# Attention and a gated MLP in one kernel: the passage from attention into the product sweeps is reordered and its loads are cut by heads

## The chip, the cores and the metric

The kernel runs on one core of a Trainium2 chip. The metric is device microseconds (us) of one execution. Three runs of the kernel before took 750.77, 751.29 and 752.87 us; the median is 751.29. The execution that the profiler recorded took 752.31 us, with a span of 750.5 us from the first to the last instruction (the other 1.8 us lie around it). All times below count from the start of that span.

## The reference

Attention with rotary position coding over 4 batches, 8 heads, 576 tokens and 64 values per head, then a gated MLP on the 2304 tokens (512 values wide, 1536 hidden).

```
q_rot, k_rot = rotate(q), rotate(k)
scores = softmax(q_rot @ k_rot.T / sqrt(64))
attn = scores @ v                                # [4, 8, 576, 64]
x = attn.transpose(0, 2, 1, 3).reshape(2304, 512)
out = (silu(x @ w_gate) * (x @ w_val)) @ w_out   # [2304, 512], float32
```

## The kernel before

**Numbers as pairs.** Each float32 operand of a matmul is split into a high part, rounded to the matmul's format by a copy on ScalarE (ACT), and a low part, the difference, made on VectorE (DVE) or GpSimd (POOL). A product is three matmuls: high by high, high by low, low by high. Such a copy and difference are a *split* (`split`).

**Stages.** Attention works through 16 head pairs, nine blocks each, until about 298 us. Each pair stores its unnormalised output (high and low halves added later) to a DRAM scratch `yd`, and each batch stores the reciprocals of its softmax sums to `rd`. The MLP works on transposed tokens, in six blocks of 384 (two halves `s` of three blocks `t`). It begins with 12 plain units of the first two hidden tiles (`UNITS`, functions `plain`, `mm`, `ev`; here u0 to u11): a unit is two chains of 12 matmuls (gate and value), each into one PSUM bank, then `ev` on ACT: Silu of the gate chain, a copy of the value chain into a staging buffer in SBUF, and a store to DRAM from ACT's queue. After the units come ten *sweeps* s (`strassen`), each with the weights of one pair of hidden tiles and three token pairs p in the order 1, 2, 0: a call of `unit` makes 7 chains of 6 matmuls instead of 8 by forming sums of operands ahead. Token pair p is blocks 2p and 2p+1; its sums are `T0`, `T1`, `T2`, its plain blocks `xa`, `xm`, `xb`. Then come the down projections (`finish`).

**The late tokens.** Blocks 0 to 3 are loaded and prepared during attention. Blocks 4 and 5 (s=1, t=1 and 2) need the last batch's last head pair. `yload(t)` loads the block's outputs into `Ya` (slot `T0h`) and `Yb` (slot `T2h`), all four head groups c at once; `rload` loads the reciprocals, spread over 64 partitions, into `R` or `R12` (slot `T2l`); `xlate(c, t)` adds, scales and splits one head group:

```
        x = self.aux()[:, 0:BK]
        ve.tensor_tensor(out=x, in0=Ya, in1=Yb, op=ALU.add)
        ve.tensor_tensor(out=x, in0=x, in1=self.R[1, t][:, c], op=ALU.mult)
        nc.scalar.copy(hi, x)
        nc.scalar.copy(Ya, x)
        ve.tensor_tensor(out=lo, in0=x, in1=r32(hi), op=ALU.subtract)
```

Units u8 and u9 read block 4, u10 and u11 block 5.

**Order.** In the MLP the order of PE, ACT, DVE and SP is the order of the code (a manual schedule); every engine runs its queue in order. `forms` (POOL) builds a token pair's sums, `forms2` (DVE) those of pair 2, from the copies of x that `xlate` leaves in `Ya`. A weight job (`Stream`, `bits`) is an Abs on ACT, six DVE operations (L721 to L726) and the next load; `J[s].sums` (POOL) and `J[s].split` make a sweep's weights. PE's chains rotate over six PSUM banks, so that a unit can start when `ev` of the unit three before has read its banks; two more banks are `aux`. The stores and loads use eight semaphore lanes; an issue waits for its lane's earlier DMA to land, and it holds its queue while it waits.

Of the kernel before, what the change touches and what calls it, by code (L numbers as in the profile page):

```python
# [14 lines left out]
ALU = mybir.AluOpType  # L15
# [503 lines left out]
class Moe:  # L519
    def __init__(self, tc, keep, pl, yd, rd, hd, wg, wv, wo, out):  # L520
        self.tc, self.nc = tc, tc.nc
        self.yd, self.rd, self.hd, self.w, self.wo, self.out = yd, rd, hd, (wg, wv), wo, out
        self.slot, self.xa, self.xm, self.xb, self.T = {}, {}, {}, {}, {}
        xs = keep.enter_context(tc.tile_pool(name="m_x", bufs=1))
        for blk in range(4):
            self.xbuf(xs, blk)
        pool = lambda name, bufs: pl.enter_context(tc.tile_pool(name=name, bufs=bufs, side="right"))
        one = pool("m_p", 1)
        self.Wb = [self.wbuf(one, 0), None]
        self.ld_p = pool("m_ld", 2)  # L530
        self.r_p = pool("m_r", 1)
# [45 lines left out]
    def open_late(self, ctx):  # L577
        def pool(name, bufs, **kw):
            return ctx.enter_context(self.tc.tile_pool(name=name, bufs=bufs, reuse_waits="tile", **kw))
        one = pool("m_late", 1)  # L580
        for blk in (4, 5):
            self.xbuf(one, blk)
        self.tbuf(one, 1)
        self.wform(one, 0)
        self.Ya = self.own(one, "T0h", [128, 2, 4, BK], FP32)
        self.Z2 = self.own(one, "T0l", [128, 2, 4, BK], FP32)
        self.Yb = self.own(one, "T2h", [128, 2, 4, BK], FP32)
        self.R12 = self.own(one, "T2l", [128, 2, 4, BK], FP32)[:, 0].rearrange("p c q -> p (c q)")
# [67 lines left out]
    def xlate(self, c, t):  # L656
        nc = self.nc
        ve = nc.vector
        hi, lo = self.xc(1, t, c)
        Ya, Yb = (Y[:, t - 1, c] for Y in (self.Ya, self.Yb))  # L660
        x = self.aux()[:, 0:BK]
        ve.tensor_tensor(out=x, in0=Ya, in1=Yb, op=ALU.add)  # L662
        ve.tensor_tensor(out=x, in0=x, in1=self.R[1, t][:, c], op=ALU.mult)
        nc.scalar.copy(hi, x)
        nc.scalar.copy(Ya, x)
        ve.tensor_tensor(out=lo, in0=x, in1=r32(hi), op=ALU.subtract)

# [110 lines left out]

    def gv(self, f, s, t):
        self.ev(f, s, t, [self.mm(f, s, t, i) for i in range(2)])  # L780

    def unit(self, fp, i, p):
# [9 lines left out]
        for k, (w, kind, x) in enumerate(PROD):  # L792
            acc = self.ch()[:, 0:BK]
            xh, xl = B[x] if kind == "B" else (Th[:, x], Tl[:, x])
            n = 0
            for c in range(2):
                for l, r in ((Wh, xh), (Wh, xl), (Wl, xh)):
                    nc.tensor.matmul(acc, l[:, w, c * 128:(c + 1) * 128], r[:, c], start=(n == 0), stop=(n == 5))  # L798
                    n += 1
# [84 lines left out]
    def hload(self, t):  # L884
        if t < FT + 2:
            self.HG[t % 2] = self.again(f"T0{'lh'[t % 2]}", [128, NFF, 2, 128], FP32, "hg")
        self.nc.sync.dma_start(out=self.HG[t % 2], in_=self.hd[1][t - FT])

    def hsplit(self, t):
# [3 lines left out]
        for z in range(0, NFF, 3):  # L893
            g, v = (G[:, z:z + 3, i] for i in range(2))
            ops.append(lambda g=g, v=v: self.nc.vector.tensor_tensor(out=g, in0=g, in1=v, op=ALU.mult))  # L895
# [45 lines left out]
def attn_swiglu(ctx: ExitStack, tc: tile.TileContext, qk, vr, wg, wv, wo, tab, out):  # L941
# [147 lines left out]
    moe.open_aux(xctx, 2)  # L1089
    J, S = plain(moe, ps)  # L1090
    mctx.close()
    pl.close()
    moe.open_mid(mctx)
    strassen(moe, J, S)
    xctx.close()
# [50 lines left out]
def plain(moe, ps):  # L1146
# [18 lines left out]
    S = Stream(moe, jobs)  # L1165
    st = {}

    def mix(p, c, Z):
        ops, st[p, c] = moe.forms(p, c, Z, po, ve)
        run(ops)  # L1170

    S.load()
    S.load()
    moe.yload(1)
    moe.rload(1, 1)
    S.sign()
    for c in range(2):
        mix(1, c, moe.Z2[:, c])
    for u, x in enumerate(UNITS):
        if u == 0:  # L1180
            moe.ev(*x, ps)
        else:
            moe.gv(*x)
        if u < 4:
            run(S.take(1, u < 3))
        if u == 1:
            run(J[0].sums(po))
            moe.yload(2)
            moe.rload(1, 2, moe.R12)
        if u in (2, 3):  # L1190
            run(st[1, u - 2])
        if u == 3:
            run(J[0].split(0, po))
            mix(0, 0, moe.again("raw0", [128, 4, BK], FP32, "Z"))
        if u == 4:
            run(J[0].split(1, po))
        if 4 <= u < 8:
            for c in range(2):
                moe.xlate(2 * u % 4 + c, u // 2 - 1)
        if u == 5:  # L1200
            mix(0, 1, moe.rz())
        if u == 7:
            moe.tagain(2)
            ops, st[2] = moe.forms2(ve, ve)
            run(ops)
            run(J[1].sums(po))
        if u == 8:
            run(st[2])
            moe.tagain(0)
        if u in (9, 10):  # L1210
            run(moe.split(ve, *(t[:, :, u - 9] for t in moe.T[0]), st[0, u - 9]))
        if u == 10:
            S.sign()
            run(S.take(1))
    return J, S

# [3 lines left out]

def strassen(moe, J, S):
    nc = moe.nc
# [88 lines left out]
```

## Time and profile before

| | us |
|---|---|
| profiled execution | 752.31 |
| its span | 750.5 |
| median of three runs | 751.29 |
| PE busy (share of the span) | 707.7 (94%) |
| DVE, POOL, ACT busy | 553.2, 460.2, 402.9 |
| first matmul of the first sweep, token pair 2 | 381.99 |

The page gives busy time per engine, then the span in 40 slices of 18.8 us, where a digit is the busy share in tenths and PEclk is the granted TensorE clock in tenths of 2.4 GHz. Then come queues, the chain of work that ended last, and groups of instructions by source line. Since PE is busy nearly everywhere, the place to look is the one where its digits fall: slices 16 to 20, from about 300 to 385 us.

### The profile page before, as it was taken

The numbers are of one execution on the slowest core, as the hardware profiler recorded it, in microseconds if no ns is written. First come the engines' busy times: TensorE is split into PE (matmuls) and PEld (weight loads), VectorE is DVE, ScalarE is ACT, GpSimd is POOL, SyncE is SP. The second block draws the span as 40 slices with busy tenths as digits, with TensorE's granted clock in tenths as the row PEclk, the third lists the DMA queues.
The fourth block names the chain that finished last, engine by engine and source line by source line (L and its number), as shares of the span: only waits on it lengthen the run. The fifth ranks groups of instructions, "written<-read, shape, count | busy, mean of one in ns | idle before, by whom it ended". The sixth has DMA issues, their size and how long they took to land.

```text
span 750.5 us, 12677 instructions
## 1 busy us (share of the span) xinstructions
PE 707.7 (94%) x4356; PEld 663.2 (88%) x4356; DVE 553.2 (74%) x895; ACT 402.9 (54%) x878; POOL 460.2 (61%) x462
## 2 busy tenths in 40 slices
PE   7699999999999998776889999999999999999997
PEld 6599999999999998775789999999999977788887
DVE  5799988888888887477686777878767885445541
ACT  2689888888889885243543342434333333333331
POOL 5696988899999846929146555676655766400000
PEclk9899999999999999987999999999999999999999
DMA  5878788889878893991236465555637965678661
GB/s 166 215 191 214 202 223 212 209 210 256 224 192 206 208 245 113 249 233 42 78 97 183 141 199 166 169 160 163 183 115 207 322 261 197 242 259 270 217 206 34
DMA packets 109873, 144.12 MB, mean 192 GB/s; under 512 B 17504, under 2 KB 86128, under 8 KB 108400
## 3 DMA queue, kind: packets, MB, share of 16 engines
q1 hardware_dynamic: 105104, 137.51, 64.0%
q10 hardware_dynamic: 4704, 5.79, 2.4%
q8 instruction: 35, 0.57, 0.3%
q14 instruction: 30, 0.25, 0.1%
HBM read 76.61 MB, written 42.54 MB: 159 GB/s over the span
## 4 chain that ended last, share of the span: by engine, by line
PE 64%; DVE 14%; DMA 11%; ACT 6%; issue 2%; POOL 2%; SPq 1%; ACTq 0%; DVEq 0%; POOLq 0%
PE ch L798 27%; PE ch L908 12%; PE pv L476 8%; PE sc L360 8%; PE tr L436 6%; DMA HF<-hf 2%; DVE nmt L375 2%; DVE aux L662 2%; PE tr L299 2%; DMA T0h<-yd 1%; ACT E L393 1%; DMA raw<-in_moe_w_gate_dram 1%; DMA T2h<-yd 1%; POOL fl L674 1%; DMA R<-rd 1%
## 5 line engine op out<-in xcount | busy, mean ns | idle before, releaser
L375 DVE TENSOR_REDUCE nmt<-sc 128x1 f32<-128x576 f32 x144 | 107.9, 751 | 21.1 <-PE sc L360 19.7
L393 ACT ACTIVATE E<-sc,nmt 128x576 f32<-128x576 f32 x128 | 97.2, 760 | 7.9 <-DVE nmt L375 7.2
L786 POOL TENSOR_TENSOR u<-u,z 128x384 f32<-128x384 f32 x30 | 30.5, 1016 | 101.1 <-DVE sg L786 101.1
L436 PE MATMUL tr<-ident,E 128*128 128x128 f32 x512 | 77.3, 274 | 0.4 <-DVE N L322 0.4
L360 PE MATMUL sc<-QK 128*128 128x288 f32 x248 | 61.5, 330 | 5.6 <-ACT ET1h L437 2.9
L801 ACT COPY c<-ch 128x384 f32<-128x384 f32 x30 | 14.4, 481 | 95.7 <-PE ch L798 52.6
L436 PEld LDWEIGHTS tr<-ident,E 128*128 128x128 f32 x512 | 61.8, 141 | 2.3 <-PE tr L299 1.4
L224 POOL TENSOR_TENSOR t<-X,tabs 128x256 f32<-128x256 f32 (+1 forms) x90 | 51.9, 598 | 15.1 <-DMA X<-in_qk_dram 7.3
L360 PE MATMUL sc<-N,QZ 128*128 128x288 f32 x248 | 54.0, 300 | 1.2 <-DMA QZ<-N 1.2
L908 PE MATMUL ch<-Oh,hh 128*128 128x512 f32 (+1 forms) x144 | 54.1, 376 | 1.0 <-ACT o L873 1.0
L437 ACT CAST ET2h<-tr 128x512 fp32r<-128x512 f32 x80 | 47.0, 587 | 13.2 <-PE tr L436 13.2
L908 PE MATMUL ch<-Oh,hl 128*128 128x512 f32 (+1 forms) x144 | 53.9, 375 | 0.0
L908 PE MATMUL ch<-Ol,hh 128*128 128x512 f32 (+1 forms) x144 | 53.9, 374 | 0.0
L438 DVE TENSOR_TENSOR ET2l<-tr,ET2h 128x512 fp32r<-128x512 f32 x80 | 52.9, 682 | 0.5 <-ACT ET2h L437 0.5
L438 DVE TENSOR_TENSOR ET1l<-tr,ET1h 128x512 fp32r<-128x512 f32 x64 | 42.8, 685 | 7.5 <-ACT ET1h L437 7.4
L228 POOL TENSOR_TENSOR rot<-rot,t 128x512 f32<-128x512 f32 (+1 forms) x45 | 45.8, 1017 | 3.5
L674 ACT CAST hh<-hg 128x384 fp32r<-128x384 f32 x44 | 22.6, 514 | 47.2 <-DVE hg L895 47.1
L786 DVE TENSOR_TENSOR sg<-ch,u 128x384 f32<-128x384 f32 x60 | 33.4, 557 | 19.1 <-PE ch L798 17.3
L674 DVE TENSOR_TENSOR hl<-hg,hh 128x384 fp32r<-128x384 f32 x44 | 24.6, 559 | 30.9 <-ACT hh L674 30.9
L360 PEld LDWEIGHTS sc<-QK 128*128 128x128 f32 x248 | 38.6, 192 | 9.8 <-ACT E L393 4.8
L437 ACT CAST ET1h<-tr 128x512 fp32r<-128x512 f32 x64 | 36.4, 597 | 18.6 <-PE tr L436 15.3
L227 POOL TENSOR_TENSOR rot<-X,tabs 128x512 f32<-128x512 f32 (+1 forms) x45 | 45.8, 1017 | 0.0
(403 smaller groups left out, 2427.5 us busy)
## 6 DMA issues: line engine op xcount, KB each, us to landing
QK<-N SPq DMA_DIRECT2D x62, 288.0 KB, 4.9
hg<-ht SPq DMA_DIRECT2D x11, 1536.0 KB, 7.7
HF<-hf SPq DMA_DIRECT2D x12, 896.0 KB, 5.2
X<-in_qk_dram SPq DMA_DIRECT2D x15, 576.0 KB, 6.9
yd<-Y SPq DMA_DIRECT2D x31, 256.0 KB, 3.2
ht<-sg SPq DMA_DIRECT2D x20, 384.0 KB, 3.5
hf<-sg SPq DMA_DIRECT2D x20, 384.0 KB, 3.6
ht<-sg SPq DMA_DIRECT2D x20, 320.0 KB, 2.9
```

The costliest lines, as they stand in the source:

```text
L224: ins = e.tensor_tensor(out=sel(t2, u), in0=sel(x, w), in1=tb(Sn, u), op=ALU.mult)
L360: nc.tensor.matmul(ps[:, g, 0:288], l, rr[:, o + g * 288:o + (g + 1) * 288], start=(x == 0), stop=(x == len(terms) - 1))
L375: nc.vector.tensor_reduce(out=nmcol, in_=ps[:, :, 0:288], axis=AX.XY, op=ALU.max, negate=True)
L393: nc.scalar.activation(out=E.rearrange("p (a b) -> p a b", a=2), in_=ps[:, :, 0:288], func=ACTF.Exp, bias=nmcol, scale=1.0, accum_out=self ...
L436: nc.tensor.transpose(ps[:, c], E[:, o + c * 128:o + (c + 1) * 128], self.ident)
L437: nc.scalar.copy(dst[0], src)
L438: nc.vector.tensor_tensor(out=dst[1], in0=src, in1=r32(dst[0]), op=ALU.subtract)
L476: nc.tensor.matmul(st["ps"][:, 0:w], VS[:, sl, :], t, start=(x == 0), stop=(x == last))
L674: return [lambda: self.nc.scalar.copy(h, f), lambda: le.tensor_tensor(out=l, in0=f, in1=r32(h), op=ALU.subtract)]
L786: add = lambda e, out, in0, in1: e.tensor_tensor(out=out, in0=in0, in1=in1, op=ALU.add)
L798: nc.tensor.matmul(acc, l[:, w, c * 128:(c + 1) * 128], r[:, c], start=(n == 0), stop=(n == 5))
L908: self.nc.tensor.matmul(ps, l[:, f], r[:, z], start=(n == 0), stop=(n == 3 * NFF - 1))
```

## The change

It changes the stretch between attention and the first sweep, in these ways.

- `yload` takes a range of head groups. Groups 0 to 2 of both late blocks are loaded first, group 3 (the last head pair) after them; the reciprocals of both blocks follow before the next weight loads. `open_late` lists the slots in another order, by which `Ya`, `Yb` stand in memory that is free early.
- `xlate` makes a list of steps: ACT copies `Ya` into the PSUM bank, and the DVE's add has that bank and `Yb` as inputs. The first steps of group c+1 stand ahead of the last ones of group c. Three of the four subtractions of `forms2` become six of half the width with x still in PSUM (L677 to L680), one stays (L709).
- `ev` has four staging buffers: two from slot `raw0`, two from `Xab`.
- The splits of token pair 0's sums (`T0`) move from the plain units into the first sweep, and its low half is two tiles. POOL's sums of pair 0 stand after the weight splits.
- The order of evictions, splits and weight jobs is new. The first sweep takes two weight jobs instead of one, after its first token pair.
- `OX` lives in the tile `R`; `hload` loads each half of a tile by a DMA of its own.

```diff
-    def yload(self, t):
+    def yload(self, t, c0, c1):
...
-                self.nc.sync.dma_start(out=Y[64 * h:64 * h + 64, t - 1], in_=src[a])
+                self.nc.sync.dma_start(out=Y[64 * h:64 * h + 64, t - 1, c0:c1], in_=src[a, :, c0:c1])
...
+        def first(c):
+            x = xs[c] = self.aux()[:, 0:BK]
+            ac.copy(x, self.Ya[:, t - 1, c])
+            tt(out=x, in0=x, in1=self.Yb[:, t - 1, c], op=ALU.add)
+            tt(out=x, in0=x, in1=self.R[1, t][:, c], op=ALU.mult)
+
+        def rest(c):
+            x = xs.pop(c)
+            hi, lo = self.xc(1, t, c)
+            ac.copy(hi, x)
+            if t == 1 or c < 2:
+                ac.copy(self.Ya[:, t - 1, c], x)
+            tt(out=lo, in0=x, in1=r32(hi), op=ALU.subtract)
+            if t == 2 and c < 2:
+                tt(out=A[:, c], in0=x, in1=A[:, c], op=ALU.subtract)
+            elif t == 2:
+                tt(out=Bl[:, c - 2], in0=x, in1=Bl[:, c - 2], op=ALU.subtract)
+                tt(out=Bl[:, c], in0=x, in1=A[:, c - 2], op=ALU.subtract)
...
+    for t in (1, 2):
+        moe.yload(t, 0, 3)
+    for t in (1, 2):
+        moe.yload(t, 3, 4)
+        moe.rload(1, t, moe.R12 if t == 2 else None)
+    for c in range(2):
+        run(moe.forms(1, c, moe.Z[c], po))
+    x1, x2 = moe.xlate(1), moe.xlate(2)
+    mm(1)
+    S.sign()
+    ev(0)
+    mm(2)
+    run(S.take(1))
+    ev(1)
+    mm(3)
+    run(S.take(1, False))
+    run(J[0].sums(po))
+    ev(2)
+    mm(4)
+    T1(0)
+    run(x1, 3)
+    ev(3)
+    mm(5)
+    run(x1)
+    ev(4)
+    mm(6)
+    T1(1)
+    S.sign()
+    run(S.take(1, False))
...
+    run(w[0])
+    ev(5)
+    mm(7)
+    run(w[1])
+    run(x2, 3)
+    ev(6)
+    mm(8)
...
+    for c in range(2):
+        run(moe.forms(0, c, Z[c], po))
+    run(x2)
+    ev(7)
+    mm(9)
+    run(moe.forms2(ve))
+    ev(8)
+    mm(10)
+    S.sign()
+    ev(9)
+    mm(11)
+    run(S.take(1))
+    ev(10)
+    run(J[1].sums(po))
+    ev(11)
...
+    at(0, 0, 1, T0(1))
+    at(0, 0, 4, T0(0))
...
-        n = {0: 1, 2: 3, 4: 3, 6: 3}.get(s, 2)
+        n = {2: 3, 4: 3, 6: 3}.get(s, 2)
```

SP's queue before, from the last weight load of attention: `T0h`, `T2h` are the two halves of the late blocks, `R` the reciprocals; the brackets name what the issue waits for (DMAHW0 to DMAHW7 are the lanes).

```order
L738 DMA raw<-in_moe_w_val_dram 128x1024 [waits DMAHW0_49,Pool_49]
L654 DMA T0h<-yd 64x4x384 [waits DMAHW4_49,DMAHW3_49,DMAHW5_49,DMAHW2_49,DMAHW6_49,DMAHW1_49,DMAHW7_49,DVE_49,Activation_49]
L654 DMA T2h<-yd 64x4x384 [waits DVE_49]
L654 DMA T0h<-yd 64x4x384
L654 DMA T2h<-yd 64x4x384 [waits DMAHW0_49]
L630 DMA R<-rd 64x4x128 [waits Pool_49]
```

The same place of SP's queue with the change:

```order
L654 DMA T0h<-yd 64x3x384 [waits DMAHW5_49,DMAHW2_49]
L654 DMA T2h<-yd 64x3x384 [waits DMAHW3_49]
L654 DMA T0h<-yd 64x3x384 [waits DMAHW4_49]
L654 DMA T2h<-yd 64x3x384 [waits DMAHW6_49]
L654 DMA T0h<-yd 64x384 [waits DMAHW0_49]
L654 DMA T2h<-yd 64x384 [waits DMAHW1_49]
L654 DMA T0h<-yd 64x384 [waits DMAHW2_49]
L654 DMA T2h<-yd 64x384 [waits DMAHW3_49]
L630 DMA R<-rd 64x4x128 [waits DMAHW4_49,Pool_49]
```

Four loads of block 4 (groups 0 to 2, not shown) stand ahead of these, right behind the weight load, and wait for lanes 4, 6, 7 and 0 and for an earlier store. The shown ones are block 5's groups 0 to 2, block 4's group 3 and the first reciprocals; before, one block came whole, and its first load waited for every lane.

ACT's queue before, from the third eviction (L766, L767 and its stores L774, L777) on; L720 is the Abs of a weight job:

```order
L720 ACTIVATE aux<-raw 128x512
L766 ACTIVATE Xab<-ch 128x3x128
L767 COPY Xab<-ch 128x3x128
L774 DMA hf<-Xab 128x256
L777 DMA ht<-Xab 128x2x256
L720 ACTIVATE aux<-raw 128x512
L674 CAST T1h<-T0l 128x4x384
```

With the change (evictions are L779, L780, stores L787, L790, `sv` and `Xab` the staging buffers):

```order
L779 ACTIVATE Xab<-ch 128x3x128
L780 COPY Xab<-ch 128x3x128
L787 DMA hf<-Xab 128x256
L790 DMA ht<-Xab 128x2x256
L694 CAST T1h<-T0l_4436 128x4x384
L665 COPY aux<-T0h 128x384 x2
L672 CAST xa2h<-aux 128x384
L674 COPY T0h<-aux 128x384
L779 ACTIVATE Xab<-ch 128x3x128
```

No weight job stands between the second and the third eviction now; the first head group of block 4 stands ahead of the fourth.

DVE's queue before, where block 4 begins:

```order
L726 TENSOR_TENSOR WF_4439<-raw,aux 128x512
L674 TENSOR_TENSOR T1l<-T0l,T1h 128x4x384
L662 TENSOR_TENSOR aux<-T0h,T2h 128x384
L663 TENSOR_TENSOR aux<-aux,R 128x384
L666 TENSOR_TENSOR xa2l<-aux,xa2h 128x384
```

With the change:

```order
L694 TENSOR_TENSOR T1l<-T0l_4436,T1h 128x4x384
L666 TENSOR_TENSOR aux<-aux,T2h 128x384
L667 TENSOR_TENSOR aux<-aux,R 128x384
L666 TENSOR_TENSOR aux<-aux,T2h 128x384
L667 TENSOR_TENSOR aux<-aux,R 128x384
L675 TENSOR_TENSOR xa2l<-aux,xa2h 128x384
```

The add now has one input from PSUM (`aux`) and one from SBUF, and group 1's add and multiplication stand ahead of group 0's subtraction.

## Rows read from the trace of the kernel before

**Rows 1.** The page's slices: busy tenths of PE, granted clock.

```profile
PE   7699999999999998776889999999999999999997
...
PEclk9899999999999999987999999999999999999999
```

**Rows 2.** Windows: length, busy us (instructions) of PE, PEld, DVE, ACT, POOL; PEclk, DMA share, GB/s.

```profile
292.00:301.00 9.00, 8.77 (x55) 8.44 (x54) 4.45 (x9) 1.96 (x5) 5.75 (x6) 1.00 0.32 98
303.20:382.00 78.80, 58.84 (x283) 53.77 (x283) 54.20 (x64) 30.12 (x54) 41.21 (x34) 0.89 0.54 147
304.00:330.00 26.00, 21.98 (x116) 21.34 (x116) 14.22 (x20) 5.54 (x10) 15.50 (x15) 0.93 1.06 263
...
343.90:353.90 10.00, 6.54 (x17) 5.23 (x18) 7.49 (x8) 3.04 (x8) 8.82 (x6) 0.50 0.15 51
420.00:450.00 30.00, 30.00 (x175) 30.00 (x174) 23.72 (x42) 13.16 (x22) 18.03 (x18) 1.00 0.58 171
```

**Rows 3.** Timeline of PE: start, us, work, [idle before and its releaser]; units u2, u3, u4, sweep.

```profile
303.20 0.44 PE L758 MATMUL ch<-xa1h,w0h 128*128 128x384 f32 x1 [0.86 <-ACT Xab L766]
...
307.47 0.34 PE L758 MATMUL ch<-xa0h,w0h 128*128 128x384 f32 x1
...
311.63 0.34 PE L758 MATMUL ch<-xm0h,w0h 128*128 128x384 f32 x1
...
381.99 0.44 PE L798 MATMUL ch<-xa2h,W0h 128*128 128x384 f32 x1 [1.62 <-DVE u L786]
```

**Rows 4.** Waits of PE, 303.2 to 382.3: total us, times, longest.

```profile
PE ch L758 <- ACT Xab L766: 10.3, 5, 3.5
```

**Rows 5.** Line L654 (late blocks' loads) on SP: ns min/median/max, first to last start.

```profile
L654 SPq EVENT_SEMAPHORE  x4: 28/28/9209, 292.3 to 301.7; - x4
L654 SPq DMA_DIRECT2D T0h<-yd x4: 585/600/679, 301.8 to 314.2; - x4
```

**Rows 6.** DMA issues, 290 to 296 us: count, KB each, median us to landing.

```profile
raw<-in_moe_w_val_dram SPq DMA_DIRECT2D x1, 512.0 KB, 3.7
```

**Rows 7.** DMA issues, 300 to 320 us.

```profile
hf<-Xab ACTq DMA_DIRECT2D x2, 384.0 KB, 7.8
R<-rd SPq DMA_DIRECT2D x2, 256.0 KB, 9.3
```

**Rows 8.** Timeline of ACT and its queue.

```profile
305.39 0.33 ACTq L774 DMA_DIRECT2D hf<-Xab  x1
318.34 0.63 ACT L720 ACTIVATE aux<-raw 128x512 f32<-128x512 f32 x1 [12.97 <-DMA raw<-in_moe_w_val_dram]
```

**Rows 9.** Groups by line and shape, 303.2 to 382: busy us, mean ns, idle before.

```profile
L662 DVE TENSOR_TENSOR aux<-T0h,T2h 128x384 f32<-128x384 f32 x8 | 12.3, 1541 | 0.0
...
L766 ACT ACTIVATE Xab<-ch 128x384 f32<-128x384 f32 x11 | 5.4, 491 | 0.0
...
L665 ACT COPY T0h<-aux 128x384 f32<-128x384 f32 x8 | 3.9, 485 | 0.0
L691 DVE TENSOR_TENSOR T0h<-T0h 128x768 f32<-128x768 f32 x4 | 3.8, 956 | 0.1
...
L674 DVE TENSOR_TENSOR T1l<-T0l,T1h 128x1536 fp32r<-128x1536 f32 x2 | 3.5, 1757 | 2.9 <-ACT T1h L674 2.9
...
L726 DVE TENSOR_TENSOR WF<-raw,aux 128x512 f32<-128x512 f32 x5 | 3.4, 686 | 0.2
...
L674 ACT CAST T1h<-T0l 128x1536 fp32r<-128x1536 f32 x2 | 2.9, 1467 | 4.5 <-DMA T2l<-rd 4.5
...
L674 ACT CAST W0h<-WF 128x1024 fp32r<-128x1024 f32 x2 | 2.1, 1042 | 0.4 <-ACT Xab L767 0.4
```

**Rows 10.** Timeline of POOL at the first late add.

```profile
333.27 3.00 POOL L674 TENSOR_TENSOR W0l<-WF,W0h 128x1024 fp32r<-128x1024 f32 x1 [13.22 <-ACT W0h L674]
```

**Rows 11.** Timeline of DVE: the first and the last of eight late adds.

```profile
333.95 2.74 DVE L662 TENSOR_TENSOR aux<-T0h,T2h 128x384 f32<-128x384 f32 x1
...
359.74 0.56 DVE L662 TENSOR_TENSOR aux<-T0h,T2h 128x384 f32<-128x384 f32 x1
```

More of the change, by code (lines that the diff above doesn't have):

```diff
@@ L653, in yload, with xlate @@
             for a, Y in enumerate((self.Ya, self.Yb)):
-                self.nc.sync.dma_start(out=Y[64 * h:64 * h + 64, t - 1], in_=src[a])
-    def xlate(self, c, t):
+                self.nc.sync.dma_start(out=Y[64 * h:64 * h + 64, t - 1, c0:c1], in_=src[a, :, c0:c1])
+    def xlate(self, t):
         nc = self.nc
[L658 to L666, printed above, removed]
+        ve, ac = nc.vector, nc.scalar
+        tt = ve.tensor_tensor
+        A, Bl = self.Ya[:, 0], self.Ya[:, 1]
+        xs = {}
+        def first(c):
[15 more added lines that the diff above has]
+                tt(out=Bl[:, c], in0=x, in1=A[:, c - 2], op=ALU.subtract)
+        ops = [lambda: first(0)]
+        for c in range(4):
+            if c < 3:
+                ops.append(lambda c=c: first(c + 1))
+            ops.append(lambda c=c: rest(c))
+        return ops
     def hicopy(self, eng, out, in_):
@@ L793, in unit @@
             acc = self.ch()[:, 0:BK]
-            xh, xl = B[x] if kind == "B" else (Th[:, x], Tl[:, x])
+            if kind == "B":
+                xh, xl = B[x]
+            else:
+                xh, xl = Th[:, x], [t[:, x] for t in Tl] if isinstance(Tl, list) else Tl[:, x]
             n = 0
             for c in range(2):
-                for l, r in ((Wh, xh), (Wh, xl), (Wl, xh)):
-                    nc.tensor.matmul(acc, l[:, w, c * 128:(c + 1) * 128], r[:, c], start=(n == 0), stop=(n == 5))
+                rh, rl = xh[:, c], xl[c] if isinstance(xl, list) else xl[:, c]
+                for l, r in ((Wh, rh), (Wh, rl), (Wl, rh)):
+                    nc.tensor.matmul(acc, l[:, w, c * 128:(c + 1) * 128], r, start=(n == 0), stop=(n == 5))
                     n += 1
@@ L833, in of @@
         if 4 <= f < 4 + NX:
+            if self.OX is None:
+                self.OX = self.r_p.tile([128, NX, DM], FP32, name="R")
             return self.OX[:, f - 4]
@@ L885, in hload @@
         if t < FT + 2:
-            self.HG[t % 2] = self.again(f"T0{'lh'[t % 2]}", [128, NFF, 2, 128], FP32, "hg")
-        self.nc.sync.dma_start(out=self.HG[t % 2], in_=self.hd[1][t - FT])
+            if t % 2:
+                G = self.again("T0h", [128, NFF, 2, 128], FP32, "hg")
+                self.HG[1] = [G[:, 0:6], G[:, 6:NFF]]
+            else:
+                self.HG[0] = [self.again(f"T0l{x}", [128, 6, 2, 128], FP32, "hg") for x in range(2)]
+        for x, G in enumerate(self.HG[t % 2]):
+            self.nc.sync.dma_start(out=G, in_=self.hd[1][t - FT, :, 6 * x:6 * x + 6])
     def hsplit(self, t):
@@ L893, in hsplit @@
         for z in range(0, NFF, 3):
-            g, v = (G[:, z:z + 3, i] for i in range(2))
+            g, v = (G[z // 6][:, z % 6:z % 6 + 3, i] for i in range(2))
             ops.append(lambda g=g, v=v: self.nc.vector.tensor_tensor(out=g, in0=g, in1=v, op=ALU.mult))
@@ L1089, in attn_swiglu @@
     moe.open_aux(xctx, 2)
-    J, S = plain(moe, ps)
+    J, S, Z = plain(moe, ps)
     mctx.close()
@@ L1165, in plain, with mm, ev @@
     S = Stream(moe, jobs)
[L1166 to L1170, printed above, removed]
+    ps, sv = {0: ps}, {}
+    def mm(u):
+        f, a, t = UNITS[u]
+        ps[u] = [moe.mm(f, a, t, i) for i in range(2)]
+    def ev(u):
+        if u % 4 == 0:
+            raw = moe.again("raw0", [128, 2, 2 * BK], FP32, "sv")
+            sv[u], sv[u + 1] = raw[:, 0], raw[:, 1]
+        elif u % 4 > 1:
+            sv[u] = moe.ld_p.tile([128, 2, BK], FP32, name="Xab").rearrange("p a q -> p (a q)")
+        moe.ev(*UNITS[u], ps.pop(u), sv.pop(u))
@@ L1172, in plain, with T1 @@
+    def T1(c):
+        run(moe.split(ve, *(t[:, :, c] for t in moe.T[1]), moe.Z[c]))
     S.load()
     S.load()
-    moe.yload(1)
-    moe.rload(1, 1)
-    S.sign()
-    for c in range(2):
[L1178 to L1214, printed above, removed]
@@ new lines, in plain @@
+    ev(4)
[3 more added lines that the diff above has]
+    run(S.take(1, False))
+    w = [J[0].split(x, po) for x in range(2)]
+    run(w[0])
[5 more added lines that the diff above has]
+    mm(8)
+    Z = [moe.r_p.tile([128, 4, BK], FP32, name="R"), moe.again("T0l0", [128, 4, BK], FP32, "Z")]
+    for c in range(2):
+        run(moe.forms(0, c, Z[c], po))
[9 more added lines that the diff above has]
+    run(S.take(1))
@@ L1227, in at, with T0, go @@
         own.setdefault((s, q, k), []).extend(f)
+    Th, Tl = moe.T[0] = [moe.again("T0h", [128, 4, 2, BK], F32R, "T0h"), [None, None]]
+    def T0(c):
+        def go():
+            Tl[c] = moe.again(f"T0l{c}", [128, 4, BK], F32R, "T0l")
+            run(moe.split(ve, Th[:, :, c], Tl[c], Z[c]))
+        return go
+    at(0, 0, 1, T0(1))
+    at(0, 0, 4, T0(0))
     for s in range(9):
```

43 lines of the change are left out of this document (18 added, 25 removed).

## The prediction

> **What bounds the kernel now.** I read the page's slices first. PE is at 9 tenths nearly everywhere, so only a stretch where that digit falls can give or take much; it falls in slices 16 to 20, where the granted clock falls too [rows 1]. The edited code runs just there. Next, windows and PE's timeline for that stretch. Unit u2 starts at 303.20, and the first sweep reaches token pair 2 at 381.99 [rows 3]: 78.8 us, from which point on both programs do the same work on PE. A plain unit of 24 matmuls takes 311.63 - 307.47 = 4.16 us at full clock, 0.1735 a matmul [rows 3]. The stretch holds ten units and 42 sweep matmuls: 41.6 + 7.3 = 48.9 us of PE work. So 29.9 us are lost: PE stands idle, or runs at the lower level (1.2 GHz; 10.0 us of it in one piece, where it did 17 matmuls [rows 2]). That is the most that the passage can give.
>
> Then the waits. The largest of PE's is for evictions by ACT, 10.3 us in five pieces [rows 4]; it is not ACT's work that is late, but what stands in front of it. One weight job's Abs kept ACT for 12.97 us on a load that landed at 318.3, with an eviction behind it [rows 8]. The load was late because the late tokens' loads were: SP stood 9.2 us, from 292.3 to 301.7, on lanes and on the last store of reciprocals, in a time of DMA share 0.32, and then everything came at once, at share 1.06 and 263 GB/s [rows 2, 5]. Last the groups by line: the late adds take 1541 ns in the mean, 0.56 us when POOL is idle [rows 9, 11].
>
> **The change, part by part.** I follow PE's next start, unit by unit.
>
> *Loads.* Block 4's groups 0 to 2 (four loads of 288 KB, 1.18 MB) go out from 292.3, where the first of them stood before [rows 5]; their lanes and stores are older, but for the fourth, which waits for the weight load beside them, 3.7 us to landing [rows 6]. At 263 GB/s they are 4.5 us of traffic taken out of the crowd [rows 2]. Block 5's groups 0 to 2 wait for the last pair's tail store and the store of reciprocals, hence till 301.7 as before [rows 5]. The first stop behind them is block 4's group 3: its second load reuses the lane of u1's store, issued at 305.39 [rows 8]. That store lands at 313.2 if it takes the 7.8 us of [rows 7]; if the DMA engines only had to move the 2.06 MB then queued (1.28 of loads, 0.79 of stores) at 263 GB/s from 301.7, at 309.6. I take the middle, 311.4. Six further issues of 0.60 [rows 5] bring the last piece of block 4's reciprocals out at 315.0. It lands 3.7 us later if queues are quiet [rows 6], 9.3 if not [rows 7]; since SP has stood still before, I take 3.7: **318.7**. Bounds: 316.9, and 326.1 (313.2 and 9.3).
>
> *Evictions.* u2's no longer stands behind a weight job, so u3 to u5 run on without a stop: u2 starts at 303.20 as before, u6 could at 303.20 + 4 x 4.16 + 0.1 = 320.0. Four staging buffers take the wait for a store's landing out of ACT's queue; the lane waits stay. Cost nil: ACT is busy 30.1 of 78.8 us [rows 2].
>
> *Block 4.* From the reciprocals on, DVE has nine operations until the last multiplication (one for group 0, then 2, 1, 2, 1, 2). A 384-wide one is 0.56 [rows 11], 0.60 with its gap. Two copies into a freed PSUM bank stand between, then the last high part and copy back, 0.49 each [rows 9]: 5.4 + 4 x 0.49 = 7.4, so ACT is through at 326.1. The copy into PSUM is not in this trace; bounds are 0.485 (L665, 384 wide, out of PSUM) and 0.63 (Abs, 512 wide, SBUF to PSUM) [rows 8, 9], at four copies on the path 0 to 0.6 us. u3's eviction stands behind group 0's high part: 318.7 + 0.6 + 3 x 0.49 = 320.8, where u6 starts (0.8 late) and ends at 325.0. u4's stands behind all of block 4: u7 starts at 326.1 + 0.49 = 326.6 and ends at 330.8.
>
> *Weight job and splits.* Behind u4's eviction (1.3 with its store's issue) ACT makes T1's second high part (1.47), the Abs (0.63) and half of W0 (1.04), and DVE T1's low part (1.76) and six operations of 0.73 (0.69 and its gap) [rows 8, 9]. u5's Silu ends at 326.1 + 1.3 + 1.47 + 0.63 + 1.04 + 0.49 = 331.0: u8 until 335.2. DVE is through at 326.1 + 1.3 + 1.47 + 1.76 + 4.4 = 335.0.
>
> *Block 5.* Group 0 needs two operations, high part, copy back, then u6's Silu: 335.0 + 1.2 + 3 x 0.49 = 337.7, u9 until 341.9 (2.5 idle). The last group's product follows after 12 operations and two copies, 335.0 + 7.2 + 1.0 = 343.2, u7's Silu after its high part at 344.2: u10 until 348.4 (2.3 idle). Then six operations (3.6), L709 (0.96), T2's second high part (1.47, by T1's row) and u8's Silu: 349.7 without a wait for POOL.
>
> *The wait for POOL.* In the rows, the first late add began while POOL's 3.00 us operation ran and ended 0.46 after it; the last, with POOL idle, took 0.56 [rows 10, 11]. In the mean an add with both inputs in SBUF cost 0.98 more than that [rows 9]. The change takes the eight adds out of this (one input is now in PSUM), but L709 and T2's low parts, which had POOL idle beside them, now stand beside pair 0's sums on POOL. I charge 0.98 for L709: 350.7, u11 until 354.9 (2.3 idle). The Trainium skill (page "SBUF — State Buffer", section "Who interferes with whom") has the rule: a VectorE instruction with two SBUF inputs and a GpSimd instruction that reads SBUF shut each other out for the whole instruction, whichever came first. The trace agrees with these two adds. By that rule L709 could wait for a whole POOL operation; with the longest one of the rows the sum would be 2.0 us longer.
>
> *First sweep.* Pair 1: 7.3 us, pair 2 at 362.2. Two T0 splits on DVE (3.5) and, over the last two token pairs (14.6 us), two weight jobs (8.7) with ten adds (5.6) make DVE nearly full, 14.3 of 14.6. I cost it at nothing: PE at 30.00 of 30.00 us with 42 DVE operations beside it [rows 2] covers sweeps with the same or more; if the banks' slack of six chains is used up, up to 3.
>
> *Clock.* PE stops for 2.5, 2.3 and 2.3 us between units of 4.16. Before, the clock was lost where PE did 17 matmuls in 10.0 us, 2.9 us of full-speed work [rows 2]. Here it works nearly two thirds of the time. Bounds: 0, and u9 to u11 at half speed, 12.5 more less the 4.6 idle that this fills, 7.9. I take 1.0, near to the lower end, because PE is so much busier than in that piece.
>
> *The rest.* `OX` in `R`, two loads for each half tile in the down projections, one weight job more in sweep 0 and one less before it: the stage after 382 is PE at full busy [rows 2] or has the same loads, so nothing, and no more than half a us either way.
>
> *The sum.* Pair 2 starts at 363.2 instead of 381.99: 18.8 us earlier. 752.3 - 18.8 = 733.5 for the profiled execution, which was 1.0 above the median of 751.29; against the median **732.5**.
>
> **The rivals.**
>
> *Half of it (R late, or the clock).* For it: 9.3 us to landing instead of 3.7 [rows 7] shifts everything from u6 on by 5.6: 738.1; low clock through u9 to u11 costs 6.9 more: 739.4. Both: 745. If block 4's early loads were held till 301.7 after all, so that the change doesn't do what it says there, the 4.5 us of traffic come back: 737. Against: both crowded figures are from a time at DMA share above 1. Chance 0.16.
>
> *PE alone paces it.* No stop after u2: 303.20 + 41.6 + 7.3 = 352.1, 29.9 earlier: 721.4. For it: I let every eviction end on the last of several waits, and took DVE's gaps in full. Against: DVE and ACT alternate on two banks. Chance 0.07.
>
> *Slower: SP's queue.* Twelve late loads stand ahead of the first reciprocals instead of four, on eight lanes; each held issue holds all behind it, and u3's and u4's evictions stand behind the reciprocals on ACT. From 318.7 on a us later is a us lost. It turns slower when they land after 337.5. Three rounds over the lanes at 9.3 us each, from 301.7, plus 9.3 for the last piece: 338.9, that is 1.4 slower with no other loss, and 4.4 with DVE's 3 in the sweep: 755.7. Against: the loads of a round overlap. Chance 0.03.
>
> **How the numbers follow.** The forecast (a gain of 15 to 26 us, 725 to 736) has 0.71, half of it 0.16, PE alone 0.07, the slower case 0.03, and 0.03 lies within the 0.3% (2.3 us) that a measurement of this kernel can tell from no change. The range of 724 to 742 takes in the bounds of the landing, most of the clock's, and of the half case what has one cause. Faster 0.94, same 0.03, slower 0.03.
>
> **What would show it.** Right: late loads from about 292; no 13 us wait of ACT for a weight load; the late adds at 0.6 us; R's last piece near 319; PE's stops short and before u6, u7, u9, u10 and u11, 8 to 11 us in all; pair 2 at about 363. Wrong: a wait above 3 us of ACT for a lane or of DVE for R; a piece of clock 0.50 between 335 and 355; PE waiting in the first sweep for DVE; a changed time after it.

## The result and the profile after

The changed kernel took 733.04 us (median of four runs, 732.30 to 734.16) against 751.28 of the kernel before beside it: ratio 0.9755, 95% interval 0.9735 to 0.9775. The profiled execution took 734.16 us, span 732.4; the forecast was 732.5. A second set of runs of the same kernel, below, gave 732.17.

The page's slices again, the rows that answer to [rows 1]:

```profile
PE   6699999999999998988999999999999999999997
...
PEclk9999999999999999999999999999999999999999
```

The dip in slices 16 to 20 is nearly gone, and the clock's with it. PE's timeline gives the stops (start, us, work, idle before it and its releaser); it answers to [rows 3, 4]:

```profile
306.06 0.44 PE L772 MATMUL ch<-xa1h,w0h 128*128 128x384 f32 x1 [1.56 <-ACT sv L779]
...
325.26 0.53 PE L772 MATMUL ch<-xm1h,w0h 128*128 128x384 f32 x1 [2.29 <-ACT Xab L779]
...
341.82 0.44 PE L772 MATMUL ch<-xa2h,w0h 128*128 128x384 f32 x1 [2.06 <-ACT Xab L779]
343.01 0.52 PE L772 MATMUL ch<-xa2h,w0l 128*128 128x384 f32 x1
...
353.40 0.44 PE L772 MATMUL ch<-xm2h,w0h 128*128 128x384 f32 x1 [1.09 <-ACT sv L779]
...
357.67 0.35 PE L812 MATMUL ch<-xa1h,W0h 128*128 128x384 f32 x1
...
364.97 0.33 PE L812 MATMUL ch<-xa2h,W0h 128*128 128x384 f32 x1
```

u2 starts at 306.06, 2.86 us later than before; three stops follow, before u6, u9 and u11, 5.4 us in all; the sweep starts at 357.67 and pair 2 at 364.97, the 7.3 us of an undisturbed pair. From u2 to pair 2 are 58.9 us, 78.8 before: 19.9 us less. The late u2 takes 2.9 of them back, and the stage behind gave 1.1 us more: 732.4 - 364.97 = 367.4 against 750.5 - 381.99 = 368.5. Together they are the profiled gain of 18.1 us.

What still holds it stands on SP, DVE and ACT (three timelines, same columns):

```profile
297.74 0.57 SPq L654 DMA_DIRECT2D T2h<-yd  x1
304.63 0.57 SPq L654 DMA_DIRECT2D T0h<-yd  x1
...
307.21 0.61 SPq L654 DMA_DIRECT2D T0h<-yd  x1
314.65 0.47 SPq L654 DMA_DIRECT2D T2h<-yd  x1
...
316.50 2.58 SPq L630 DMA_DIRECT2D R<-rd  x4
```

```profile
314.25 2.60 DVE L694 TENSOR_TENSOR T1l<-T0l,T1h 128x1536 fp32r<-128x1536 f32 x1 [1.37 <-ACT T1h L694]
...
323.35 0.57 DVE L667 TENSOR_TENSOR aux<-aux,R 128x384 f32<-128x384 f32 x1 [6.03 <-DMA R<-rd]
...
349.73 1.72 DVE L709 TENSOR_TENSOR T0h<-T0h 128x768 f32<-128x768 f32 x1
351.37 5.89 DVE L694 TENSOR_TENSOR T2l<-T0h,T2h 128x1536 fp32r<-128x1536 f32 x2
```

```profile
308.25 0.33 ACTq L787 DMA_DIRECT2D hf<-sv  x1
...
347.32 0.50 ACT L779 ACTIVATE Xab<-ch 128x384 f32<-128x384 f32 x1
```

u1's store goes out at 308.25; SP's issue behind its lane stands from 307.8 to 314.65; the reciprocals of block 4 follow, and DVE waits 6.03 us for them. That is the chain of the prediction, at nearly its times. Nothing is left of ACT's 12.97 us in [rows 8]. By groups (columns as in [rows 9], window 306.06 to 365), the late adds:

```profile
L666 DVE TENSOR_TENSOR aux<-aux,T2h 128x384 f32<-128x384 f32 x8 | 4.5, 561 | 2.8 <-ACT aux L665 2.8
```

561 ns each, 1541 before. Last, the clock, in three windows (columns as in [rows 2]):

```profile
325.00:328.00 3.00, 2.74 (x9) 2.74 (x10) 1.92 (x4) 1.85 (x5) 0.00 (x0) 0.58 1.19 251
341.00:345.00 4.00, 3.17 (x12) 3.18 (x13) 3.33 (x7) 2.42 (x6) 3.92 (x4) 0.69 0.58 199
343.00:345.00 2.00, 2.00 (x8) 2.00 (x8) 1.86 (x4) 0.87 (x3) 1.92 (x2) 0.50 0.58 197
```

After the stops before u6 and u9 PE runs on the lower level (1.2 GHz) for a few us: u6 takes 331.17 - 325.26 = 5.9 us and u9 6.05, instead of 4.16, 3.6 us in all.

### The profile page after: what moved, and what is told of

It reads as the page before. It is cut to its first block, busy times and chain, and to the rows that moved or that the text cites. A ratio compares the mean times of both kernels' runs of the same rounds, so it can differ in the third digit from the quotient of the medians.

```text
span 732.4 us, 12724 instructions
## 1 busy us (share of the span) xinstructions
PE 703.4 (96%) x4356; PEld 662.1 (90%) x4356; DVE 550.8 (75%) x898; ACT 405.9 (55%) x884; POOL 465.5 (64%) x462
## 4 chain that ended last, share of the span: by engine, by line
PE 73%; DVE 10%; DMA 6%; ACT 5%; SPq 2%; issue 1%; POOL 1%; ACTq 0%; DVEq 0%; POOLq 0%
PE ch L812 30%; PE ch L929 13%; PE pv L476 9%; PE sc L360 8%; PE tr L436 6%; PE ch L880 3%; DMA HF<-hf 2%; ACT E L393 2%; DVE nmt L375 1%; PE tr L299 1%; DMA X<-in_qk_dram 1%; ACT N L318 1%; DMA hf<-sv 1%; DMA QZ<-N 1%; DVE HF L870 1%
## 5 line engine op out<-in xcount | busy, mean ns | idle before, releaser
L375 DVE TENSOR_REDUCE nmt<-sc 128x1 f32<-128x576 f32 x144 | 108.0, 752 | 21.1 <-PE sc L360 19.9
```

The lines of the kernel that those rows point to most:

```text
L375: nc.vector.tensor_reduce(out=nmcol, in_=ps[:, :, 0:288], axis=AX.XY, op=ALU.max, negate=True)
```

## The experiments

Twelve runs. "Passage" is from u2's first matmul to pair 2's in the run's own trace; it leaves out chance ahead of the passage (in old_order, sbuf_adds and r12_first it holds about 1.5 us that u2, 5.7 to 5.8 us long, lost to a lower clock). It comes from one trace of each kernel; the two of the changed kernel differ by 0.3. The ratio is to the kernel before, run beside it.

| run | us, median | ratio, 95% | passage |
|---|---|---|---|
| before | 751.28 | 1 | 78.8 |
| changed | 733.04 | 0.9755 (0.9735 to 0.9775) | 58.9 |
| after_again | 732.17 | 0.9737 (0.9717 to 0.9758) | 59.2 |
| before_early | 747.61 | 0.9960 (0.9945 to 0.9975) | 75.5 |
| before_psum | 749.60 | 0.9964 (0.9949 to 0.9978) | 76.7 |
| old_order | 739.25 | 0.9841 (0.9803 to 0.9880) | 66.6 |
| t0_back | 737.29 | 0.9806 (0.9781 to 0.9831) | 63.5 |
| two_staging | 730.41 | 0.9716 (0.9691 to 0.9740) | 58.7 |
| sbuf_adds | 730.65 | 0.9712 (0.9686 to 0.9739) | 58.2 |
| loads_late | 732.53 | 0.9756 (0.9738 to 0.9774) | 60.9 |
| whole_loads | 729.49 | 0.9715 (0.9698 to 0.9733) | 57.3 |
| r12_first | 727.92 | 0.9684 (0.9658 to 0.9710) | 56.8 |
| raws_first | 728.55 | 0.9688 (0.9673 to 0.9704) | 55.6 |
| all_three | 725.22 | 0.9667 (0.9644 to 0.9690) | 52.7 |

### The base: is the late start part of the change?

> The changed kernel once more, unchanged, for a base beside the other runs: its profile had the passage start 2.9 us later than before (u2 at 306.06 instead of 303.20), while the runs with small edits start it at 302.6 to 304.2. Theory A (the late start is chance, from the stage ahead of the passage): u2 at 302.5 to 304.5, 730 to 732, and the wait of DVE for the reciprocals still 6 us, since two staging buffers and four then have the same time. Theory B (the early loads bring it): u2 near 306 and 733.

u2 at 303.00, pair 2 at 362.24; DVE waits 6.9 us for the reciprocals. Theory A on the start and on the wait; the time, 732.17, lies between the two. The passages agree to 0.3 us. Why the start wanders (302.2 to 306.1 over all traces, behind the same attention) stays open.

### One part alone, in the kernel before

```
 before_early: the order in which late tiles are given out
-Ya  Z2  Yb  R12  WF
+WF  Z2  R12  Ya  Yb
 before_psum: xlate
+nc.scalar.copy(x, Ya)
-ve.tensor_tensor(out=x, in0=Ya, in1=Yb, op=ALU.add)
+ve.tensor_tensor(out=x, in0=x, in1=Yb, op=ALU.add)
```

> The kernel before, with one thing changed: the late tokens' tiles are given out in another order, so that block 4's tiles don't lie over ones that attention still uses, and its four whole loads can go out from about 292 instead of 301.7. Nothing else of the change. Against 751.3 us. Theory A: reciprocals and weight loads move up by the four loads (2.4 us of issue and 1.6 MB of traffic), the weight load that landed at 318.3 lands near 313, and with the clock lost there it is 744 to 747, a third of the gain. Theory B (early loads are the gain): 733 to 740. Theory C (the order of the engines is the gain): 749 to 751.

3.3 us, in passage and time alike: a little less than theory A's least. ACT's waits in this trace, the first line of them (total us, times, longest), show why the rest does not follow: the weight load still lands late.

```profile
ACT aux L720 <- DMA raw<-in_moe_w_val_dram: 9.7, 1, 9.7
```

> The kernel before, with the eight late adds taking one half from PSUM, where ACT copies it first. Nothing else of the change. Against 751.3 us. Theory A (the adds wait for POOL's operations): the mean of an add falls from 1.54 to about 0.6, and of the 7.5 us saved on DVE part lies on the path, less the copies of 0.49 on ACT: 746 to 750. Theory B (it is no gain, since the copy is one more step in a chain that alternates between ACT and DVE): 751 to 754.

Theory A by time, 2.1 us of passage. But of the 7.8 us that the eight adds got shorter, most came back as waiting for the copy (by groups on DVE, 303 to 362):

```profile
L663 DVE TENSOR_TENSOR aux<-aux,T2h 128x384 f32<-128x384 f32 x8 | 4.5, 561 | 5.6 <-ACT aux L662 5.6
```

### One part undone, in the changed kernel

```
 old_order (block 5's loads moved behind the two weight loads as well)
-run(S.take(1, False)); sums; ev(2); mm(4); T1(0)
+run(S.take(1)); sums; ev(2); mm(4); T1(0); run(S.take(1, False))
 ...
-T1(1); S.sign(); run(S.take(1, False))
+T1(1)
 t0_back: T0(1) before ev(10), T0(0) behind it, no longer in the sweep
 two_staging: sv[u] from ld_p (two buffers) for every unit
 sbuf_adds: first(c)
-ac.copy(x, Ya[c]);  tt(out=x, in0=x, in1=Yb[c], op=ALU.add)
+tt(out=x, in0=Ya[c], in1=Yb[c], op=ALU.add)
```

> The changed kernel, with the third weight job back where it stood: its Abs on ACT ahead of u2's eviction, its six operations on DVE ahead of block 4's, its load behind block 4's reciprocals, block 5's loads behind that. Block 4 still loads early by groups. Against 733.0 us. Theory A (PE waits for whatever is last of loads and DVE; the order of ACT alone is worth little once the loads are early): the load lands near 315, u2's eviction 3 to 4 us later than now, block 4 starts no later than now since its reciprocals go out sooner: 730 to 735. Theory C (u2's eviction ahead of the weight job is the main gain): half of the 18 us goes back, 739 to 743, with ACT waiting over 5 us for the weight load.

Theory C. ACT's timeline names three waits in a row, and PE's the stop that they make:

```profile
317.91 0.64 ACT L734 ACTIVATE aux<-raw 128x512 f32<-128x512 f32 x1 [10.68 <-DMA raw<-in_moe_w_val_dram]
...
323.13 1.47 ACT L694 CAST T1h<-T0l 128x1536 fp32r<-128x1536 f32 x1 [3.80 <-DMA T0h<-yd]
...
330.67 0.48 ACT L665 COPY aux<-T0h 128x384 f32<-128x384 f32 x1 [5.69 <-DVE WF L740]
```

```profile
333.06 0.69 PE L772 MATMUL ch<-xm1h,w0h 128*128 128x384 f32 x1 [9.61 <-ACT Xab L779]
```

The weight load holds u2's eviction; and even where it has landed, the job's six operations on DVE stand ahead of block 4. The passage is 7.5 us longer, 6 without the 1.5 that u2 lost to the clock in this trace. So the place of the third weight job, with the order of block 5's loads that went back with it and was not tried apart, is worth some 6 us, the largest single part.

> The changed kernel with the first pair's two splits back ahead of the sweep, one in front of u10's eviction, one behind it. Against 733.0 us. Theory A (the first sweep hides them, the passage doesn't): DVE's two low parts of 1.8 us and ACT's two high parts of 1.5 stand in front of the evictions that free the sweep's first banks: 735 to 738, with PE stopping at the start of the sweep. Theory B (they were hidden in the passage as well): 733.

Theory A: 4.2 to 4.5 us of passage more. PE stops at the sweep's start, behind ACT, which stood on a split that waited for POOL's sums, and then runs on at a granted clock of 0.65 (360.4 to 364.0):

```profile
360.44 0.44 PE L812 MATMUL ch<-T1h,W0h 128*128 128x384 f32 x1 [1.78 <-ACT Xab L779]
```

```profile
357.98 1.47 ACT L694 CAST T0h<-Z 128x1536 fp32r<-128x1536 f32 x1 [3.70 <-POOL Z L700]
```

> The changed kernel with two staging buffers instead of four. Against 733.0 us. Theory A (as predicted, nothing): u2's eviction waits for u0's store, out at 306.4 and 6.4 us to landing, so it comes up to 4 us later, but ACT and DVE wait for block 4's reciprocals till 323.3 anyway: 732 to 734. Theory B (four buffers are needed for the new order): the later evictions wait for stores as well, 736 to 740.

Theory A for the passage: 58.7 against 58.9 and 59.2. ACT does wait 3.4 and 1.4 us for stores, in the shadow of the 6.0 us for the reciprocals. Why the time came out below the expected range is open; the passage, where the buffers are used, is the same. Four buffers bring nothing here.

> The changed kernel, with the eight late adds reading both halves from SBUF again, without ACT's copy into PSUM. Against 733.0 us. Theory A (such an add waits for what POOL is doing): block 4's four run while POOL has nothing, and save 1 to 2 us of copies on the path; block 5's four run beside pair 0's sums on POOL and cost about 1 us more each, as before: 733 to 736. Theory B (they wait for whole POOL operations of 3 to 7 us): 738 or more. Theory C (the copies are the dearer of the two): 730 to 732.

Theory C by the median, 730.65; the ratio's interval overlaps that of after_again, so I read it as no gain from the copy, not as a sure loss. The trace points to a loss of some 2 us: without what u2 lost to the clock the passage is 56.6. In the kernel before the copy was worth 2 us. The adds' group (DVE, 303 to 362) says why: where they now stand POOL is often idle. Three of the eight, from 321.53 on, found it so and took 0.56 to 0.57; the dearest, the second line, lies ahead of the wait for the reciprocals, where it costs nothing.

```profile
L665 DVE TENSOR_TENSOR aux<-T0h,T2h 128x384 f32<-128x384 f32 x8 | 7.9, 982 | 0.1
...
314.56 2.21 DVE L665 TENSOR_TENSOR aux<-T0h,T2h 128x384 f32<-128x384 f32 x1
```

### SP's queue

```
 changed:     y4[0:3], y5[0:3], y4[3], R4, y5[3], R5, raw, raw
 whole_loads: y4, R4, y5, R5, raw, raw
 loads_late:  R4, y4, y5, R5, raw, raw
 r12_first:   y4, R4, R5, y5, raw, raw
 raws_first:  y4, R4, raw, raw, y5, R5
 all_three:   y4, R4, R5, raw, raw, y5, and the adds as in sbuf_adds
```

(y4, y5: the loads of blocks 4 and 5; R4, R5: their reciprocals; raw: the third and fourth weight load.)

> The changed kernel, with each late block loaded whole again: four loads of block 4, its four loads of reciprocals, four of block 5, its reciprocals. It stands against 733.0 us of the changed kernel. Theory A (SP's queue is the rest of the loss): with the loads by groups, block 5's loads and a store's lane stand ahead of block 4's reciprocals, which land at 323.3; DVE waits 6.0 us for them. Here nothing but the store of reciprocals holds them: issued from about 305.5, landed near 313, DVE's wait gone, units from u6 on up to 6 us earlier: 727 to 729. Theory B (loading by groups is what lets block 4 start early): the first group waits for the whole block, block 5 and block 4 crowd each other: 734 to 737.

> The changed kernel, with block 4's reciprocals first in SP's queue, then block 4 and block 5 whole, so that no load of late tokens goes out before the store of reciprocals. Against 733.0 us. Theory A (what counts is when the last of block 4's inputs lands; DVE is free for it at 317.3): reciprocals out from 305.5, block 4 out by 310.5, landed near 316: 727 to 730, with no early load at all. Theory B (taking 1.2 MB out of the crowd before 302 is worth its 4.5 us of traffic or more): block 4 lands after 321 and the time is 733 to 738.

whole_loads: 3 us faster than the changed kernel, 1.6 to 1.9 of them in the passage, just above theory A's upper end. The cut by groups, with the order that went with it (block 5's first loads ahead of block 4's reciprocals), is a loss; the two were not tried apart. The reciprocals are there at 314.04, as expected, but a new wait takes over. DVE first, then ACT:

```profile
314.04 0.56 DVE L667 TENSOR_TENSOR aux<-aux,R 128x384 f32<-128x384 f32 x1 [0.47 <-DMA R<-rd]
...
322.35 0.57 DVE L666 TENSOR_TENSOR aux<-aux,T2h 128x384 f32<-128x384 f32 x1 [6.22 <-ACT aux L665]
```

```profile
315.77 0.50 ACT L780 COPY Xab<-ch 128x384 f32<-128x384 f32 x1
321.47 0.33 ACTq L787 DMA_DIRECT2D hf<-Xab  x1
321.83 0.48 ACT L665 COPY aux<-T0h 128x384 f32<-128x384 f32 x1 [5.57 <-DMA T2h<-yd]
```

The copy at 321.83 did not wait for tokens, which had landed long before. The issue of u3's store ahead of it went out 5.2 us after its eviction: its lane's DMA before was block 5's last load. loads_late fell between the theories: block 4 began at 315.84, on time and without any early load, and then ACT stood on the same store until 324.17, for a lane of another load, so that u7 waited 5.55 us. Block 4's first multiplication, at 316.44, came 2.4 us later than in whole_loads; sending it early is worth no more than that here. In both runs ACT then stood for a lane, until 321.47 and 324.17, so the 3.6 us between the two passages are the lanes' doing.

> The changed kernel with block 4 loaded whole, as in the run before, but block 5's six small loads of reciprocals now stand ahead of its four large loads. Nothing is moved on ACT, DVE, POOL or PE. Against 729.5 us of the run with block 5's loads first. Theory A (a lane that ACT's store of u3 shares with block 5's last load held ACT, 5.6 us, from 316.3 to 321.5): in the new order that store's lane belonged to a load of reciprocals that lands by 314, so ACT goes on at once, block 4 is done 5 us earlier and so are u7 and what follows: 724 to 726. Theory B (ACT's copy really waited for late tokens, or DVE's chain of block 5 is the bound): 728 to 731.

Only SP's order differs, and the store goes out at once:

```profile
317.21 0.50 ACT L780 COPY Xab<-ch 128x384 f32<-128x384 f32 x1
317.77 0.34 ACTq L787 DMA_DIRECT2D hf<-Xab  x1
...
330.33 0.63 ACT L734 ACTIVATE aux<-raw 128x512 f32<-128x512 f32 x1 [4.78 <-DMA raw<-in_moe_w_val_dram]
```

So the wait was the lane's; but the time, 727.92, is in theory B's range, for a reason that neither named: the weight loads, now last in SP's queue (issued at 318.97), hold ACT 4.78 us.

> The changed kernel with SP's queue in the order: block 4 whole, its reciprocals, the two weight loads, block 5 whole, its reciprocals. Nothing moved on the other engines. Against 727.9 us of the run with block 5's reciprocals first. Theory A (there ACT stood 4.8 us on the third weight job's load, landed at 330, behind all of block 5 in SP's queue, and DVE's chain for u9 to u11 stood behind it): that load lands by 316, DVE is through the job at 331.6 instead of 335.2, sweep and end 3.6 earlier: 723.5 to 725.5. Theory B (block 5's late tokens or reciprocals then come too late, or DVE's chain is the bound anyway): 727 to 730.

That wait is gone, yet 728.55 is theory B's: u3's and u4's stores wait for lanes again, 1.9 and 1.8 us by the rows below: the passage, 55.6, is no shorter than r12_first's 56.8 less the 1.6 that its u2 lost to the clock.

```profile
318.24 0.48 ACT L665 COPY aux<-T0h 128x384 f32<-128x384 f32 x1 [1.86 <-DMA raw<-in_moe_w_val_dram]
...
325.52 1.48 ACT L694 CAST T1h<-T0l 128x1536 fp32r<-128x1536 f32 x1 [1.76 <-DMA T2h<-yd]
```

> The changed kernel with SP's queue in the order: block 4 whole, its reciprocals, block 5's reciprocals, the two weight loads, block 5 whole; and the late adds read both halves from SBUF again, without the copy. Against 727.9 us of the run with block 5's reciprocals first and 728.6 us of the one with the weight loads first. Theory A (what is left in those two are ACT's waits: 4.8 us for the third weight job's load in the one, 1.9 and 1.8 us for lanes of two stores in the other; here the stores' lanes belong to small early loads and the weight load lands near 321, before ACT wants it; and the copies cost the path about 2 us): 722.5 to 725. Theory B (DVE's chain for block 5 is the bound already): 727 to 729, or more if block 5's tokens, now last, land after 331.

725.22, just above theory A's range: 7 us faster than the changed kernel. What of it is the order and what the missing copy, this run does not separate. After u2 no stop before u9, three small ones from there:

```profile
333.07 0.44 PE L771 MATMUL ch<-xa2h,w0h 128*128 128x384 f32 x1 [0.42 <-ACT Xab L778]
339.19 0.44 PE L771 MATMUL ch<-xm2h,w0h 128*128 128x384 f32 x1 [1.69 <-ACT Xab L778]
...
355.98 0.33 PE L811 MATMUL ch<-xa2h,W0h 128*128 128x384 f32 x1
```

## Why the prediction was right

The mechanism held. The forecast for the passage was 60.0 us (363.2 - 303.20); the two traces have 58.9 and 59.2. That the first median came within 0.5 us of the forecast is in part luck: in the profiled execution a start 2.86 us late, which no term had, stands against a passage and a stage behind it that were each 1.1 us shorter than put. Starts, the changed kernel's less the 2.86 us of its late u2:

| | predicted | changed, less 2.86 | after_again |
|---|---|---|---|
| u6 | 320.8 | 322.4 | 322.6 |
| u7 | 326.6 | 328.3 | 328.5 |
| u9 | 337.7 | 339.0 | 339.1 |
| u10 | 344.2 | 345.0 | 345.2 |
| u11 | 350.7 | 350.5 | 350.7 |
| sweep | 354.9 | 354.8 | 354.9 |
| pair 2 | 363.2 with 1.0 for the clock | 362.1 | 362.2 |

*Loads.* Right in kind: first stop, its lane and its order. u1's store took 6.4 us against the 6.0 taken. The last piece was put at 318.7; DVE's multiplication came at 323.35, which is 320.5 less the late start, and 320.65 in after_again. Mis-sized by 1.9: 1.2 of it because the piece took about 4.9 us to land (issued near 318.5), not 3.7, the rest in the lane and the issues ahead of it.

*Evictions.* u3 to u5 ran without a stop, as put. "Cost nil" for the buffers holds, and two would have done.

*Block 4, weight job, block 5.* Taken 7.4 from the reciprocals to the end of block 4; measured 330.73 - 323.35 = 7.4. The 1.6 us of the late landing go on to u9 at 1.3, and are made up by u11, where the chain of DVE and ACT was about 1.4 shorter than summed.

*Stops and clock.* Here two terms were mis-sized against each other. Predicted: 9.7 us of stops and 1.0 of low clock; measured: 5.4 and 3.6. u7 and u10 did not stop, though the evictions that they need were no earlier than put. u4's Silu ended at 331.12 and u7's at 347.82 (328.3 and 344.96 less 2.86; 326.6 and 344.2 put), but u6 and u9, at the lower clock, needed just as long, so that u7 and u10 start at once:

```profile
330.61 0.51 ACT L779 ACTIVATE sv<-ch 128x384 f32<-128x384 f32 x1
331.17 0.44 PE L772 MATMUL ch<-xm1h,w0h 128*128 128x384 f32 x1
...
347.87 0.44 PE L772 MATMUL ch<-xm2h,w0h 128*128 128x384 f32 x1
```

whole_loads shows the same step without the low clock: u9 at full clock, then a stop, and 6.04 us from u9's start to u10's against 6.05 here.

```profile
337.68 0.44 PE L772 MATMUL ch<-xa2h,w0h 128*128 128x384 f32 x1 [2.05 <-ACT Xab L779]
343.72 0.44 PE L772 MATMUL ch<-xm2h,w0h 128*128 128x384 f32 x1 [1.61 <-ACT Xab L779]
...
337.68:342.10 4.42, 4.42 (x24) 4.11 (x24) 3.19 (x7) 2.48 (x6) 4.26 (x4) 1.00 0.34 118
```

So a unit whose successor waits for an eviction anyway can run slowly for nothing, and the 1.0 us for the clock should not have stood beside the stops: without it the sum has pair 2 at 362.2, as measured (the late landing and the shorter chain, above, cancel).

*The wait for POOL.* Charged 0.98 for L709; it took 1.72 against 0.956, 0.77 more. POOL's rows beside it:

```profile
347.79 1.86 POOL L700 TENSOR_TENSOR Z<-xa0h,xa0l 128x768 f32<-128x768 f32 x1
349.59 1.04 POOL L700 TENSOR_TENSOR Z<-xm0h,xm0l 128x384 f32<-128x384 f32 x1
350.56 1.77 POOL L700 TENSOR_TENSOR Z<-xb0h,xb0l 128x384 f32<-128x384 f32 x1
```

L709 started at 349.73, 0.14 after a POOL operation, and ended 0.82 after that one's end; POOL's next operation took 1.77 instead of the 1.0 of its like. By the rule of the Trainium skill (page "SBUF — State Buffer", section "Who interferes with whom") each waits for the whole of the other's instruction, and the trace agrees: the operation in front of L709 was one of 1.04 us, not the 3.00 that the prediction's longer sum took. (The first late add of [rows 10, 11] ended 0.42 after POOL's operation, not 0.46.) T2's two low parts, 5.89 against 3.5 for T1's [rows 9], show the interference too, behind u11's eviction, where it cost PE nothing. What the prediction missed is that moving the adds to where POOL is idle does over half of what the copy does (982 ns instead of 1541), and that the copy is paid for on ACT.

*First sweep.* "At nothing" holds to 0.1 us; the same splits ahead of it cost 4.2 to 4.5 (t0_back).

*The rest.* Nothing, half a us either way, was put; 1.1 came: PE's 1.0 us for an output copy in the down projections is not in the trace after.

Three signs missed. PE's stops were to come before five units, 8 to 11 us in all; they came before three, 5.4 us. A piece of clock 0.50 between 335 and 355 was to be a sign of being wrong; it came (343 to 345), and cost nothing, as shown above. And one sign was set against the working itself: "a wait above 3 us [...] of DVE for R" would be wrong, it said, but with R at 318.7 and DVE free when the trace has it, at 314.4 (317.3 less 2.9), 4 us of waiting go with the sum. The wait came (6.03), and told of a reserve rather than of an error: SP's queue, which the rival "SP's queue" saw only as a danger. Its order alone was worth 3 to 5 us (whole_loads, r12_first, raws_first), and 7 with the copies gone as well (all_three).

The parts, each alone, in us of passage: the third weight job's place 6 (with block 5's loads), the splits in the sweep 4.2 to 4.5, earlier whole loads 3.3, adds through PSUM 2 (in the kernel before; none or a loss in the changed one), four buffers 0, loads by groups (with their order) -1.6 to -1.9. They are not additive: they were measured in different kernels, and each moves the others' waits.

## What to carry to other kernels

Where several engines issue DMAs, ask of every issue which DMA holds its lane: a store on a busy compute engine may stand for a load that it has nothing to do with, and order in another engine's queue cures it. When a wait falls, read the next profile for the new first wait before crediting the edit: here three orders of one queue each uncovered another. And undo each part of a bundled change by itself: of six, one was a loss, one was nothing, and one lost its worth beside the others.

## What the runs showed of the hardware

A 384 KB load from `yd` took some 10 us to land in a crowd (issued at 311.21 in whole_loads, its lane free at 321.47, at a DMA share of 1.10), against 5.8 and 6.3 us in the median for 288 KB loads in the changed kernel. TensorE's granted clock was at the lower level for 3.7 us after a stop of 2.29 us, and in u9 for some 3 us after one of 2.06, while before u11 a stop of 1.09 left it at full speed. The length of the stop does not decide it alone: in whole_loads stops of 2.44 us before u7 and 2.05 before u9 left the clock at 1.00. Why is open. An add of two SBUF tiles took 0.56 us beside an idle POOL; with one input in PSUM it took 0.56 in every place, whatever POOL did.
